# A fused attention and two-MLP kernel: other SBUF places for the last output copies of the first MLP and for two weight loads, and another slot for its last products

## The chip, the cores and the metric

The kernel runs on 1 core of one Trainium2 chip. The metric is the device time of one execution in microseconds (us). The kernel before takes 1925.05 us, the median of 3 runs (1924.63 to 1925.43).

## The reference, cut to what matters

```python
x = attention(q, k, v)                  # k and v mean-pooled by 8 along the sequence
x = x.transpose(0, 2, 1, 3).reshape(4608, 512)
h = sigmoid(x @ w_gate) * (x @ w_val)   # 512 -> 1536
x = h @ w_out                           # 1536 -> 512, first MLP
h = elu(x @ w_in2)                      # 512 -> 2048
out = h @ w_out2                        # 2048 -> 512, second MLP
```

There are 8 batches of 8 heads, 576 positions and 64 dimensions a head, so 4608 tokens of 512. The weights arrive as 64-bit floats and are read as pairs of 32-bit words.

## The kernel before, in words

All of it is one program, written in the order in which each engine runs it. Every engine is a queue: an instruction that waits holds up all that is behind it on that engine. A matrix product is made of three products of two-part numbers (high with high, high with low, low with high), since each operand is split into a high part (ScalarE, L93) and a rest (GpSimd or VectorE, L94).

**Blocks of the first MLP.** The tokens go in 12 blocks of 384 (`n`). A block has 12 groups of hidden columns (`c`). For a group TensorE makes the gate product and the value product (12 matmuls each, L501), ScalarE the sigmoid, VectorE the product of both (L513), ScalarE and GpSimd split it into `g`, and TensorE adds the output product of the group before (12 matmuls, L520) into four PSUM tiles `acc`. The two PSUM tiles `gv` are used in turn, so a gate or value product starts only after L513 has read the product two before it. At the block's end `flush_y` (L531) copies the four `acc` tiles, two on ScalarE and two on VectorE, to SBUF tiles `yo` and stores each to DRAM.

**Narrowing the weights.** In the first block the weights of the first MLP are still being made: 36 pieces (`Job`), three for each group (gate, value, out). A piece is loaded raw (L125, L131), its magnitude is taken on ScalarE (`open_to`, L188), VectorE narrows it in four passes (L106, L110, L116, L120), and ScalarE and GpSimd split it. `convert` (L195) does one step: it issues loads two pieces ahead, opens the next piece, runs two passes of one piece and two of the next in turn, and splits the piece before. A raw piece lies in one of two places of the tag `raw`, or, for an even piece number up to 30, in one of the 12 places of the tag `wo`, which the finished output weights fill in the end (L179 to L182). The narrowed form in work lies in one of three places of the tag `nt` (L143). From the second block on, the weights of the second MLP are narrowed in the same way in the gaps (`prepared`, L217) and stored to DRAM; that is over before the last block, and the `nt` places are next used by `flush_o` (L904).

**The second MLP.** It runs over 6 pairs of blocks (`s`), 8 column groups (`q`) and 7 products (`k`) each; such a step is a slot, counted through by `slot`. `product` (L845) adds 6 matmuls into one of two PSUM banks; `ORDER` says which bank and whether it is opened anew. `behind` (L868) reads the bank after each product: a bank can be added to or opened again only when its reader is done. After product 0 ScalarE copies the bank to `p`; product 2 goes on in that bank; after product 2 come ScalarE's Relu and Exp (with a table load the first time) and VectorE's L863, and product 4 opens the bank again; after product 4 VectorE makes `c` (L880), ScalarE Relu and Exp of it, VectorE L863 and L883, and the next group's product 0 opens the other bank behind L883. Between the products TensorE runs matmuls from the list `fill` (`filler`, L840): in the first group the 12 output products (L520) of the first MLP's last group, later those of the second MLP (L896). Work in the dictionary `due` is called at the end of its slot; the last `flush_y` is due in slot 4. Three of the four places of the tag `row`, from which `flush_y` takes its `yo` tiles (L89, L533), are held by `t_p1`, `t_u2` and `t_u3` (L825) there.

Of the kernel before, what the change touches and what calls it, by code (L numbers as in the profile page):

```python
# [9 lines left out]
F32 = mybir.dt.float32  # L10
# [14 lines left out]
def fused_kernel(  # L25
# [25 lines left out]
    NT, DM = out.shape  # L51
    F1 = w_gate.shape[1] // 2
    F2 = w_in2.shape[1] // 2
    P = 128
# [4 lines left out]
    C1 = F1 // P  # L59
    C2 = F2 // P  # L60
    NB = 384
    NBLK = NT // NB
# [9 lines left out]
    act = ctx.enter_context(tc.tile_pool(name="act", bufs=1))  # L72
# [12 lines left out]
    def raw_tile(name):  # L85

        return act.tile([P, DM, 2], I32, name=name, tag="raw", bufs=2)

    def row_tile(name, n=512):  # L89
        return act.tile([P, n], F32, name=name, tag="row", bufs=4)  # L90
# [79 lines left out]
    def upto(step, n):  # L170
        n = min(n, len(jobs))
        while count[step] < n:
            yield jobs[count[step]]
            count[step] += 1

    def fetch_to(n):
        for job in upto("fetch", n):
            i = count["fetch"]
            if i % 2 or i > 3 * C1 - 6:  # L179
                job.raw = raw_tile("rw")  # L180
            else:
                job.raw = wts.tile([P, DM, 2], I32, name="rwo", tag="wo", bufs=C1)  # L182
            job.load(job.raw)
# [346 lines left out]

    def flush_y(n, acc):  # L531
        for m in range(KD):
            t = row_tile("yo", NB)  # L533
            if m % 2:
                nc.vector.tensor_copy(out=t, in_=acc[m])
            else:
                nc.scalar.activation(out=t, in_=acc[m], func=AF.Copy)
            nc.sync.dma_start(out=y_dram[n][:, m], in_=t)
# [66 lines left out]
    with tc.manual_schedule():  # L605
# [101 lines left out]
        def low():  # L707
            for f in lows:
                f()
            lows.clear()  # L710
# [27 lines left out]
        def load_pair(q):  # L738
            wp[q] = [wts.tile([P, 7, 256], F32R, name=f"wr{q}{i}", tag="wg", bufs=C1) for i in range(2)]
            for i in range(2):  # L740
                nc.sync.dma_start(out=f32(wp[q][i]), in_=w_dram[q][:, i])

        def load_wo2(c):
            if c < C1:
                wo2[c] = wts.tile([P, 2, DM], F32R, name=f"w2o{c}", tag="wo", bufs=C1)
            elif c % 2 == 0:
                t = wts.tile([P, 2, 2, DM], F32R, name=f"w2o{c}", tag="wg", bufs=C1)
                wo2[c], wo2[c + 1] = t[:, 0], t[:, 1]
            nc.sync.dma_start(out=f32(wo2[c]), in_=wo2_dram[c])
# [6 lines left out]
        for n in range(NBLK):  # L756
# [3 lines left out]
            for c in range(C1):  # L760
# [49 lines left out]
                if pend is not None:  # L810
                    pn, pacc, pg, pc = pend
# [26 lines left out]
        fill = []  # L838

        def filler(n):  # L840
            for f in fill[:n]:
                f()
            del fill[:n]

        def product(k, q, flip, s):  # L845
            b, w, a, opens = ORDER[k]
            n = 0
            for j in range(2):
                for a_w, a_x in PASSES:
                    nc.tensor.matmul(  # L850
                        bank[b ^ flip], lhsT=wp[q][a_w][:, w, j * P:(j + 1) * P], rhs=form_tile(s, a)[j][:, a_x],
                        start=opens and n == 0, stop=n == 5, skip_group_check=True,
                    )
                    n += 1
# [13 lines left out]
        def behind(k, flip, g):  # L868
            src = bank[ORDER[k][0] ^ flip]
            u2 = t_u2  # L870
            if k == 0:
                nc.scalar.activation(out=t_p1, in_=src, func=AF.Copy)
            elif k == 1:
                nc.vector.tensor_tensor(out=u2, in0=t_p1, in1=src, op=ALU.add)  # L874
            elif k == 2:
                elu("c11", src, g)
            elif k == 3:
                nc.vector.tensor_tensor(out=t_u3, in0=t_p1, in1=src, op=ALU.add)
            elif k == 4:
                nc.vector.tensor_tensor(out=c_22, in0=t_u3, in1=src, op=ALU.add)  # L880
                elu("c22", c_22, g)
            elif k == 5:
                nc.vector.tensor_tensor(out=t_u3, in0=t_u3, in1=src, op=ALU.subtract)  # L883
                elu("c21", t_u3, g)
            else:
                nc.vector.tensor_tensor(out=u2, in0=u2, in1=src, op=ALU.add)
                elu("c12", u2, g)
# [3 lines left out]
        def to_out(acc, g, q, c, i, opens, closes):  # L891

            e, t = OUT_OF[c]

            def one(p, a_g, a_w):
                return lambda: nc.tensor.matmul(  # L896
                    acc[t + i], lhsT=g[c][:, a_g, i * P:(i + 1) * P], rhs=wo2[2 * q + e][:, a_w],
                    start=opens and p == 0, stop=closes and p == 2,
                )

            return [one(p, *x) for p, x in enumerate(PASSES)]

        def flush_o(t, acc):
            o = act.tile([P, DM], F32, name="po", tag="nt", bufs=3)  # L904
            if t % 2:
                nc.vector.tensor_copy(out=o, in_=acc)
            else:
                nc.scalar.activation(out=o, in_=acc, func=AF.Copy)
            nc.sync.dma_start(out=out[t * P:(t + 1) * P, :], in_=o)

        pn, pacc, pg, pc = pend
        fill += y_steps(pacc, pg, pc)
        NS = NBLK // 2
        prev = None
        flip = 0
        due = {4: [lambda: flush_y(pn, pacc)]}
        slot = 0
        for s in range(NS):
            for q in range(NQ):
                g = {  # L920
                    c: pool.tile([P, 2, NB], F32R, name="g" + c, tag=t, bufs=n)
                    for c, pool, t, n in (
                        ("c11", act, "g", 2), ("c12", mlp2[0], "g12", 1),
                        ("c21", mlp2[0], "g21", 1), ("c22", mlp2[0], "g22", 1),
                    )
                }
                if prev is not None:
                    ps_, pq, pg = prev
                    if pq == 0:
                        acc = [  # L930
                            ps.tile([P, DM], F32, name="oacc", tag="gv" if i < 2 else "acc", bufs=2 if i < 2 else 4)
                            for i in range(2 * TPB)
                        ]
                    if pq < NQ - 1:
                        for c in ("c11", "c22", "c21", "c12"):
                            for i in range(TPB):
                                fill += to_out(acc, pg, pq, c, i, pq == 0 and c in ("c11", "c22"), False)
                    else:
                        for n, i in enumerate((3, 4, 5, 0, 1, 2)):
                            for c in ("c11", "c12") if i < TPB else ("c21", "c22"):  # L940
                                fill += to_out(acc, pg, pq, c, i % TPB, False, c in ("c12", "c22"))
                            due.setdefault(slot + n + 1, []).append(
                                lambda t=ps_ * 2 * TPB + i, a=acc[i]: flush_o(t, a)
                            )
                for k in range(7):
                    product(k, q, flip, s)
                    filler(-(-len(fill) // max(1, (7 if slot > 6 else 5) - k)))
                    todo, later[:] = later[:], []
                    for f in todo:
                        f()  # L950
                    behind(k, flip, g)
                    low()
                    if k == 0 and (s > 0 or q > 0) and not (s == NS - 1 and q == NQ - 1):

                        load_pair((q + 1) % NQ)
                    if s == 0 and k == 1:
                        for c in {1: (10, 11), 2: (12, 13), 3: (14, 15)}.get(q, ()):
                            load_wo2(c)
                    if s + 1 < NS:
                        if q == 1 and k == 0:  # L960
                            load_raw(s + 1)
                        if q in (3, 4):
                            form_early(s + 1, (q - 3) * 7 + k)
                        if q == NQ - 1 and k == 4:

                            for i in range(8):
                                due.setdefault(slot + i, []).append(
                                    lambda i=i, s=s: form(s + 1, 3 + i // 2, i % 2)
                                )
                    for f in due.pop(slot, ()):  # L970
                        f()
                    slot += 1
                prev = (s, q, g)
                flip ^= 1
# [40 lines left out]
```

## Time and profile before

| what | value |
|---|---|
| median of 3 runs | 1925.05 us |
| the profiled execution, its own time | 1925.16 us |
| its span, first to last instruction | 1923.4 us |
| TensorE busy (matmul) | 1836.2 us, 95% |
| VectorE busy | 886.8 us, 46% |
| ScalarE busy | 810.7 us, 42% |
| GpSimd busy | 509.5 us, 26% |
| mean granted TensorE clock | 0.979 of full |
| DMA queue of the transfers | 211.84 MB, 32.4% of 16 engines |

Names are the engines' short forms: PE is TensorE, PEld its weight loads, DVE is VectorE, ACT is ScalarE, POOL is GpSimd, SP issues the DMAs. In a row of the timeline the first number is the start in us from the start of the span, the second the time from the first to the end of the last instruction that the row merges, `xN` their number, and the bracket the idle time before it and what ended it. Matmuls overlap, so six of them in 1.20 us are followed by the next after less than that.

### The profile page before, as it was taken

What the parts mean: (1) busy time and instruction counts of PE and PEld (TensorE: products, weight loads), DVE (VectorE), ACT (ScalarE), POOL (GpSimd) and SP (SyncE); (2) the same over time, 40 slices, a digit from 0 to 9 for tenths busy, and PEclk for the clock granted to TensorE, in tenths of its full rate; (3) what the DMA queues carried; (4) which work ended last, traced back from release to release, by engine and by line L of the source; (5) the groups of instructions that cost most, each with busy time, mean ns of one, the idle gap of its engine ahead of it and who ended that gap; (6) DMA issues with size and microseconds to landing.
All of it is one profiled execution on the core that took longest, in us unless ns stands there. A gap on an engine that the chain in (4) does not pass through costs nothing.

```text
span 1923.4 us, 25809 instructions
## 1 busy us (share of the span) xinstructions
PE 1836.2 (95%) x9996; PEld 1733.8 (90%) x9996; DVE 886.8 (46%) x1455; ACT 810.7 (42%) x1575; POOL 509.5 (26%) x523
## 2 busy tenths in 40 slices
PE   4676999999999999999999997999999999999999
PEld 3666999999999999999999997999999999999997
DVE  7987354554445544554422132544344344443432
ACT  3543344344444344444433224454454444544543
POOL 4444222222213132123222112222222222222222
PEclk7887999999999999999999999999999999999999
DMA  8332123232232322242210425334343343434330
GB/s 225 114 117 86 50 91 107 82 94 72 86 99 71 127 80 80 89 124 98 73 28 1 159 77 193 124 134 175 121 190 116 117 179 115 156 139 151 151 116 33
DMA packets 115771, 213.49 MB, mean 111 GB/s; under 512 B 43968, under 2 KB 72640, under 8 KB 115648
## 3 DMA queue, kind: packets, MB, share of 16 engines
q1 hardware_dynamic: 115648, 211.84, 32.4%
q8 instruction: 78, 1.28, 0.3%
q14 instruction: 45, 0.37, 0.1%
HBM read 169.87 MB, written 41.94 MB: 110 GB/s over the span
## 4 chain that ended last, share of the span: by engine, by line
PE 88%; DVE 7%; DMA 2%; ACT 2%; issue 1%; POOL 0%; SPq 0%; ACTq 0%; DVEq 0%; POOLq 0%
PE gv L501 28%; PE oacc L896 21%; PE bank L850 18%; PE acc L520 14%; PE xv L481 2%; PE ats L414 2%; PE atv L481 2%; DVE nt L106 1%; DVE ks L354 1%; DVE nt L116 1%; PE atq L404 1%; DVE nt L120 1%; PE att L454 1%; DMA rkv<-in_k_dram 1%; DVE nt L110 1%
## 5 line engine op out<-in xcount | busy, mean ns | idle before, releaser
L501 PE MATMUL gv<-x,wg 128*128 128x384 f32 x3456 | 651.8, 342 | 24.4 <-DVE sg L513 19.9
L501 PEld LDWEIGHTS gv<-x,wg 128*128 128x128 f32 x3456 | 607.0, 191 | 30.2 <-ACT wo L93 12.6
L896 PE MATMUL oacc<-w2o,gc 128*128 128x512 f32 x1728 | 452.9, 393 | 0.4 <-POOL gc L94 0.4
L896 PEld LDWEIGHTS oacc<-w2o,gc 128*128 128x128 f32 x1728 | 320.0, 188 | 48.4 <-POOL gc L94 0.8
L850 PE MATMUL bank<-form,wr 128*128 128x384 f32 x1728 | 354.0, 340 | 9.7 <-DVE u L883 8.3
L94 POOL TENSOR_TENSOR g<-sg,g 128x384 fp32r<-128x384 f32 x144 | 155.1, 1077 | 724.2 <-ACT g L93 724.2
L850 PEld LDWEIGHTS bank<-form,wr 128*128 128x128 f32 x1728 | 315.4, 188 | 32.9 <-DVE u L883 8.6
L520 PE MATMUL acc<-g,wo 128*128 128x384 f32 x1728 | 330.3, 339 | 2.0 <-POOL g L94 2.0
L520 PEld LDWEIGHTS acc<-g,wo 128*128 128x128 f32 x1728 | 304.4, 190 | 6.1 <-POOL g L94 3.4
L513 DVE TENSOR_TENSOR sg<-sg,gv 128x384 f32<-128x384 f32 x144 | 79.1, 549 | 313.8 <-PE gv L501 311.6
L94 POOL TENSOR_TENSOR gc<-ea,gc 128x384 fp32r<-128x384 f32 x96 | 98.0, 1021 | 301.5 <-ACT gc L93 297.3
L94 POOL TENSOR_TENSOR gc<-eb,gc 128x384 fp32r<-128x384 f32 x96 | 97.9, 1020 | 266.6 <-ACT gc L93 246.1
L509 ACT ACTIVATE sg<-gv 128x384 f32<-128x384 f32 x144 | 70.7, 491 | 199.9 <-PE gv L501 195.4
L93 ACT ACTIVATE g<-sg 128x384 fp32r<-128x384 f32 x144 | 75.6, 525 | 174.2 <-DVE sg L513 174.2
L859 ACT ACTIVATE ea<-bank 128x384 f32<-128x384 f32 x48 | 23.6, 492 | 158.5 <-PE bank L850 158.5
L94 DVE TENSOR_TENSOR pt<-att,pt 128x512 fp32r<-128x512 f32 x72 | 34.8, 486 | 114.7 <-ACT pt L93 114.7
L863 DVE SCALAR_TENSOR_TENSOR ea<-ea,bank 128x384 f32<-128x384 f32 x48 | 26.6, 555 | 118.0 <-ACT ea L860 118.0
L859 ACT ACTIVATE eb<-c 128x384 f32<-128x384 f32 x48 | 25.2, 525 | 129.6 <-DVE c L880 129.6
L93 ACT ACTIVATE gc<-eb 128x384 fp32r<-128x384 f32 x96 | 50.4, 525 | 56.3 <-DVE eb L863 33.0
L93 ACT ACTIVATE gc<-ea 128x384 fp32r<-128x384 f32 x96 | 50.5, 526 | 55.4 <-DVE ea L863 55.4
L874 DVE TENSOR_TENSOR u<-p,bank 128x384 f32<-128x384 f32 x48 | 26.6, 555 | 98.7 <-PE bank L850 97.3
L509 ACT ACT_TABLE_LOAD x34 | 43.6, 1283 | 49.8 <-PE gv L501 49.6
(104 smaller groups left out, 1872.5 us busy)
## 6 DMA issues: line engine op xcount, KB each, us to landing
wr<-wd SPq DMA_DIRECT2D x96, 896.0 KB, 6.3
rw<-in_moe_w_out_dram SPq DMA_DIRECT2D x23, 512.0 KB, 3.7
yd<-yo SPq DMA_DIRECT2D x48, 192.0 KB, 2.1
r<-yd SPq DMA_DIRECT2D x24, 384.0 KB, 8.4
out_dram<-po SPq DMA_DIRECT2D x36, 256.0 KB, 2.0
rw<-in_moe_w_in_dram SPq DMA_DIRECT2D x16, 512.0 KB, 4.5
wd<-rw SPq DMA_DIRECT2D x16, 512.0 KB, 3.5
wod<-rw SPq DMA_DIRECT2D x16, 512.0 KB, 2.8
```

What stands on the lines that cost most here:

```text
L93: nc.scalar.activation(out=dst_hi, in_=src, func=AF.Copy)
L94: eng.tensor_tensor(out=dst_lo, in0=src, in1=f32(dst_hi), op=ALU.subtract)
L414: nc.tensor.matmul(a[o:o + n, j // 2, (j % 2) * w:(j % 2 + 1) * w], lhsT=qt[:, j * P + o:j * P + o + n], rhs=kbd[b % 2][:, j * w:(j + 1) * w],
L481: nc.tensor.matmul(d[j][:, o:o + w], lhsT=vb[:m, a_w].rearrange("p e d -> p (e d)"), rhs=p[:m, a_p, j + e, o:o + w], start=(e == 0 and a_w ...
L501: nc.tensor.matmul(d, lhsT=w[:, i, a_w, j], rhs=x[:, a_x, j], start=(j == 0 and a_w == 0 and a_x == 0), stop=(j == KD - 1 and a_w == 1),)
L509: nc.scalar.activation(out=sg, in_=gps, func=AF.Sigmoid)
L513: nc.vector.tensor_tensor(out=sg, in0=sg, in1=vps, op=ALU.mult)
L520: return lambda: nc.tensor.matmul(acc[m], lhsT=wo[c][:, a_w, m * P:(m + 1) * P], rhs=g[:, a_g], start=(c == 0 and a_w == 0 and a_g == 0), ...
L850: nc.tensor.matmul(bank[b ^ flip], lhsT=wp[q][a_w][:, w, j * P:(j + 1) * P], rhs=form_tile(s, a)[j][:, a_x], start=opens and n == 0, stop= ...
L859: nc.scalar.activation(out=e, in_=src, func=AF.Relu, scale=-1.0)
L863: nc.vector.scalar_tensor_tensor(out=e, in0=e, scalar=-1.0, in1=src, op0=ALU.add, op1=ALU.max)
L896: return lambda: nc.tensor.matmul(acc[t + i], lhsT=g[c][:, a_g, i * P:(i + 1) * P], rhs=wo2[2 * q + e][:, a_w], start=opens and p == 0, st ...
```

## The change

Three edits: the even pieces 32 and 34 are also loaded into places of `wo`; in the flush of the last block the second to fourth copy go to `nt` places; the 12 output products that lay between the products 0 to 4 of the second MLP's first group all stand behind product 3, and the flush is due in slot 3 and not 4. After slot 6 `filler` counts as before.

```diff
     def fetch_to(n):
         for job in upto("fetch", n):
             i = count["fetch"]
-            if i % 2 or i > 3 * C1 - 6:
+            if i % 2:
                 job.raw = raw_tile("rw")
             else:
                 job.raw = wts.tile([P, DM, 2], I32, name="rwo", tag="wo", bufs=C1)
...
     def flush_y(n, acc):
         for m in range(KD):
-            t = row_tile("yo", NB)
+            if n == NBLK - 1 and m:
+                t = act.tile([P, DM], F32, name="yn", tag="nt", bufs=3)[:, :NB]
+            else:
+                t = row_tile("yo", NB)
...
-        due = {4: [lambda: flush_y(pn, pacc)]}
+        due = {3: [lambda: flush_y(pn, pacc)]}
...
                 for k in range(7):
                     product(k, q, flip, s)
-                    filler(-(-len(fill) // max(1, (7 if slot > 6 else 5) - k)))
+                    filler(len(fill) if slot == 3 else -(-len(fill) // (7 - k)) if slot > 6 else 0)
```

On SP, the queue that issues the loads, these are the loads of the pieces 31 to 35 in the first block and the first of the second MLP. Before:

```order
L125 DMA rw<-in_moe_w_val_dram 128x4x256
L131 DMA rw<-in_moe_w_out_dram 128x1024
L125 DMA rw<-in_moe_w_gate_dram 128x4x256
L125 DMA rw<-in_moe_w_val_dram 128x4x256
L131 DMA rw<-in_moe_w_out_dram 128x1024
L125 DMA rw_1499<-in_moe_w_in_dram 128x4x256
```

The same loads in the changed kernel:

```order
L125 DMA rw<-in_moe_w_val_dram 128x4x256
L131 DMA rwo<-in_moe_w_out_dram 128x1024
L125 DMA rw<-in_moe_w_gate_dram 128x4x256
L125 DMA rwo<-in_moe_w_val_dram 128x4x256
L131 DMA rw<-in_moe_w_out_dram 128x1024
L125 DMA rw_1499<-in_moe_w_in_dram 128x4x256
```

The order is the same; pieces 32 and 34 go to `rwo`, a place of `wo`, so that the five loads use two places of each tag in turn.

On PE, at the start of the second MLP, this is what stands from the second of the old gaps on (`form_9758` is the operand of product 2, `form_9812` of product 3, `form_9862` of product 4). Before:

```order
L520 MATMUL acc<-g,wo_1342 128x384 x3
L850 MATMUL bank_9984<-form_9758,wr_9501 128x384 x2
L850 MATMUL bank_9984<-form_9758,wr_9502 128x384
L850 MATMUL bank_9984<-form_9758,wr_9501 128x384 x2
L850 MATMUL bank_9984<-form_9758,wr_9502 128x384
L520 MATMUL acc<-g,wo_1342 128x384 x2
L850 MATMUL bank_9985<-form_9812,wr_9501 128x384 x2
L850 MATMUL bank_9985<-form_9812,wr_9502 128x384
L850 MATMUL bank_9985<-form_9812,wr_9501 128x384 x2
L850 MATMUL bank_9985<-form_9812,wr_9502 128x384
L520 MATMUL acc<-g,wo_1342 128x384 x2
L850 MATMUL bank_9984<-form_9862,wr_9501 128x384 x2
```

The same place in the changed kernel, from product 2 on:

```order
L853 MATMUL bank_9984<-form_9758,wr_9501 128x384 x2
L853 MATMUL bank_9984<-form_9758,wr_9502 128x384
L853 MATMUL bank_9984<-form_9758,wr_9501 128x384 x2
L853 MATMUL bank_9984<-form_9758,wr_9502 128x384
L853 MATMUL bank_9985<-form_9812,wr_9501 128x384 x2
L853 MATMUL bank_9985<-form_9812,wr_9502 128x384
L853 MATMUL bank_9985<-form_9812,wr_9501 128x384 x2
L853 MATMUL bank_9985<-form_9812,wr_9502 128x384
L520 MATMUL acc<-g,wo_1342 128x384 x12
L853 MATMUL bank_9984<-form_9862,wr_9501 128x384 x2
```

The products 0 to 3 now stand one behind another, and all 12 output products stand between product 3 and product 4. Lines behind `flush_y` have numbers higher by 3.

On DVE, in the same group, from the first L863 on. Before:

```order
L863 SCALAR_TENSOR_TENSOR ea<-ea,bank_9984 128x384
L878 TENSOR_TENSOR u_9988<-p_9986,bank_9985 128x384
L880 TENSOR_TENSOR c_9989<-u_9988,bank_9984 128x384
L535 COPY yo<-acc 128x384 x2
L863 SCALAR_TENSOR_TENSOR eb<-eb,c_9989 128x384
L883 TENSOR_TENSOR u_9988<-u_9988,bank_9985 128x384
```

The same place in the changed kernel:

```order
L866 SCALAR_TENSOR_TENSOR ea<-ea,bank_9984 128x384
L881 TENSOR_TENSOR u_9988<-p_9986,bank_9985 128x384
L538 COPY yn<-acc 128x384 x2
L883 TENSOR_TENSOR c_9989<-u_9988,bank_9984 128x384
L866 SCALAR_TENSOR_TENSOR eb<-eb,c_9989 128x384
L886 TENSOR_TENSOR u_9988<-u_9988,bank_9985 128x384
```

The two flush copies move from behind `c` to ahead of it. On ScalarE its two copies move likewise, from behind the Exp of `eb` to ahead of the Relu of `eb`. GpSimd's queue is unchanged.

## Rows read from the trace of the kernel before

**Rows 1.** Windows: start:end, length, busy time (instructions) by engine, PE clock, DMA share, GB/s
```profile
191.80:1148.90 957.10, 955.11 (x5689) 940.37 (x5688) 419.11 (x674) 372.21 (x701) 225.31 (x248) 1.00 0.27 85
1160.20:1168.40 8.20, 0.01 (x1) 0.00 (x0) 2.03 (x4) 0.91 (x2) 0.00 (x0) 0.77 0.21 75
1168.40:1172.30 3.90, 3.83 (x12) 3.50 (x13) 1.49 (x4) 2.73 (x6) 2.02 (x2) 0.61 0.95 328
1172.30:1923.40 751.10, 746.67 (x3691) 671.84 (x3690) 305.07 (x552) 344.54 (x700) 192.86 (x189) 1.00 0.37 139
```
**Rows 2.** Waits of PE, 1172 us to the end: us in total, times, longest
```profile
PE oacc L896 <- POOL gc L94: 0.4, 1, 0.4
```
**Rows 3.** Waits of all engines, 160 to 191.8 us
```profile
PE gv L501 <- DVE sg L513: 9.6, 3, 7.9
ACT nt L188 <- DMA rw<-in_moe_w_gate_dram: 5.5, 1, 5.5
```
**Rows 4.** Timeline, 130 to 143 us, a round of three pieces in the first block
```profile
130.54 0.41 DVE L106 TENSOR_SCALAR nt<-nt 128x512 f32<-128x512 f32 x1
...
131.92 0.69 DVE L116 SCALAR_TENSOR_TENSOR nt<-rw,nt 128x512 int32<-128x512 int32 x1
132.29 1.46 POOL L94 TENSOR_TENSOR wg<-nt,wg 128x512 fp32r<-128x512 f32 x1 [5.23 <-ACT wg L93]
132.53 1.50 DVE L106 TENSOR_SCALAR nt<-nt 128x512 f32<-128x512 f32 x1
...
135.58 2.32 PE L501 MATMUL gv<-x,wg 128*128 128x384 f32 x12 [1.18 <-DVE sg L513]
...
139.15 1.07 DVE L373 TENSOR_REDUCE vs<-v 128x64 f32<-128x512 f32 x1
...
142.91 0.69 DVE L116 SCALAR_TENSOR_TENSOR nt<-rwo,nt 128x512 int32<-128x512 int32 x1
```
**Rows 5.** Timeline, 163 to 190 us, the end of the first block
```profile
163.64 2.66 PE L520 MATMUL acc<-g,wo 128*128 128x384 f32 x12
...
169.22 0.69 DVE L116 SCALAR_TENSOR_TENSOR nt<-rw,nt 128x512 int32<-128x512 int32 x1
...
176.24 4.18 PE L501 MATMUL gv<-x,wg 128*128 128x384 f32 x12 [7.86 <-DVE sg L513]
...
189.54 2.35 PE L501 MATMUL gv<-x,wg 128*128 128x384 f32 x12 [1.25 <-DVE sg L513]
```
**Rows 6.** Timeline, 1148 to 1183 us, the start of the second MLP
```profile
1148.98 1.20 PE L850 MATMUL bank<-form,wr 128*128 128x384 f32 x6
...
1152.10 1.20 PE L850 MATMUL bank<-form,wr 128*128 128x384 f32 x6
...
1156.45 1.33 PE L850 MATMUL bank<-form,wr 128*128 128x384 f32 x6 [1.41 <-DVE ea L863]
...
1157.96 2.24 PE L850 MATMUL bank<-form,wr 128*128 128x384 f32 x12
...
1166.92 0.56 DVE L535 COPY yo<-acc 128x384 f32<-128x384 f32 x1 [4.52 <-DMA yd<-yo]
...
1167.86 0.55 DVE L883 TENSOR_TENSOR u<-u,bank 128x384 f32<-128x384 f32 x1
...
1168.47 2.29 PE L850 MATMUL bank<-form,wr 128*128 128x384 f32 x6 [8.26 <-DVE u L883]
...
1172.36 1.22 PE L850 MATMUL bank<-form,wr 128*128 128x384 f32 x6
...
1172.88 0.47 ACT L872 ACTIVATE p<-bank 128x384 f32<-128x384 f32 x1
...
1174.57 1.23 PE L850 MATMUL bank<-form,wr 128*128 128x384 f32 x6
...
1179.01 1.23 PE L850 MATMUL bank<-form,wr 128*128 128x384 f32 x6
...
1182.51 0.55 DVE L883 TENSOR_TENSOR u<-u,bank 128x384 f32<-128x384 f32 x1
```

## The prediction, as recorded before the changed kernel ran

> **What bounds the kernel now.** I read the windows by stage first, then the waits of TensorE, then the timeline at the two places where TensorE stands still. Between 191.8 and 1148.9 us TensorE is busy 955.1 of 957.1 us at the full granted clock, and from 1172.3 us to the end 746.7 of 751.1 us [rows 1]; in that last stretch the waits of TensorE that the trace names come to 0.4 us [rows 2]. So in these two stretches, nine tenths of the span, only fewer or shorter matmuls would help, and the change takes none away. It also means that whatever time is won before such a stretch is kept: everything behind it is in TensorE's pace and moves forward as a whole. What is left are two holes, and each edit lies at one of them.
>
> The first hole is the end of the first block. There ScalarE, opening piece 33, waits 5.5 us for its raw load [rows 3]; the trace has three such waits, one each for the pieces 33, 34 and 35. These pieces share two raw places, and a load can go out only when the piece two before has had its last pass. TensorE waits at the end of that chain, 9.6 us in three waits, 7.9 of it in one [rows 3].
>
> The second hole is the start of the second MLP: TensorE waits 1.41 us for L863 ahead of product 4 and 8.26 us for L883 ahead of the next group's product 0 [rows 6]. In the second wait VectorE does almost nothing (2.0 of 8.2 us busy, [rows 1]): its second copy for the flush stands 4.52 us waiting for a store [rows 6]. The four copies share one place of `row`, the other three being held, so copy and store alternate, and L863 and L883 stand behind the copies on VectorE.
>
> **The loads (first edit).** Pieces 32 and 34 go to `wo`, so load 33 no longer waits for piece 31 and load 35 no longer for piece 33; loads then go out as far ahead as in the rounds before. The places exist: ten of twelve are held by output weights and by piece 30 when load 32 is issued. Up to the pass L116 at 169.22 us nothing moves, because VectorE gets there on other work (the transposed probabilities come just ahead of it). From there I take the pace of an undisturbed round. In such a round TensorE's product that waits for L513 starts 135.58 − 131.92 = 3.66 us after the pass L116 [rows 4]. At the end of the block the same pair stands 176.24 − 169.22 = 7.02 us apart [rows 5]; this product moves to 172.88. A whole round takes 142.91 − 131.92 = 10.99 us, with a pooling step of 1.07 us that does not come again here, so 9.92 [rows 4]: the last piece's L116 starts at 179.14. From it to TensorE's last gate product it is 3.66 less the two passes of a following piece, which there is not (1.50 and about 0.41, as the long and the short pass of rows 4): 1.75, or 1.1 more if a pass of the last piece is held up by GpSimd. That gives 180.9 to 182.0. TensorE itself needs, from 172.88 on, a product at the slow pace (4.18), an output product (2.66) and a gate product (2.35, [rows 5]), which ends at 182.1 with all overlaps left out. I take 182.0. It now starts at 189.54 [rows 5]: **7.5 us**.
>
> Bounds: if every one of the 14 passes from there took the long 1.50 us, with 0.55 for L513, the last product could start only near 191.5, a loss of 2 us; if none did, TensorE's own products with their overlaps still fill the time to about 181.5, a gain of 8.0. I take the undisturbed round, since the same order of passes is measured there with the long and the short ones in it.
>
> A pass beside GpSimd shows what can be late next: L106 took 0.41 us alone and 1.50 us when it started behind a 1.46 us GpSimd split [rows 4]. The Trainium skill (SBUF — State Buffer, section Who interferes with whom) says that a VectorE instruction with two SBUF inputs, or one in a two-port mode, and a GpSimd instruction that reads SBUF do not share the port pair, but that the later waits for the earlier. By that rule the closer pace puts more passes behind splits; with all of them held the sum would lose these 7.5 us and 2 more, with the measured round it keeps them.
>
> **The twelve products and the flush (second and third edit).** Counted on from the first product at 1148.98 us, which nothing moves. Six matmuls take 2.24 − 1.20 = 1.04 us in a row, one 0.17 [rows 6]. Without fill product 2 starts at 1151.06; it needs the copy of product 0, which is done at 1150.18 + 0.47, so it does not wait. From product 2 to product 4 it is 1156.45 − 1152.10 = 4.35 us, the chain of Relu, table load, Exp and L863 [rows 6]. That chain stays, and sets product 4 to 1155.41. Beside it TensorE has the products 2 and 3 and all twelve, 4 × 1.04 = 4.16 us: its wait shrinks from 1.41 to 0.2 us. So the early products gain 1.04 us, and two more output matmuls are already done.
>
> The four copies now have four places: the three of `nt` are idle (no instruction between 960 us and the flush names them), the fourth is the free one of `row`. They stand ahead of `c` on VectorE and ahead of the Relu of `eb` on ScalarE. Two of 0.56 us behind L863 and L878 end near 1156.8; `c` cannot start before product 4 has ended, 1156.7, so they cost 0.1 us. From product 4 to L883, without a flush between them, it is 1182.51 − 1179.01 = 3.50 us, one group later [rows 6]; L883 then runs 1159.0 to 1159.56, and the next group's product 0 follows at 1159.6 instead of 1168.47. TensorE runs out of work at 1155.41 + 3 × 1.04 = 1158.5, so a wait of 1.1 us stays.
>
> Late next is ScalarE's copy of that product: it ends 4.94 us after L883 (1173.35 against 1168.41), in an order that stays, so at 1164.5, and product 2 of that group follows at 1164.54; TensorE could be there at about 1164.2. Now it starts at 1174.57 [rows 6]: **10.0 us**. Of this the low clock behind the long wait is a part: with 0.61 granted, product 0 and its fill of six took 3.89 us up to 1172.36, the next product and its fill of five at the full clock 2.21 [rows 1, 6].
>
> Bounds: at most both waits and the slow start go, 1.41 + 8.26 + 1.5 = 11.1 us; at least, were the copies held as before, 1.1 us.
>
> The transfers behind the flush on SP (weights of the group after next, the next rows of the first MLP) go out some 9 to 10 us earlier, and so does their use; they keep about the same time to land.
>
> **Sum.** 7.5 + 10.0 = 17.5 us from the profiled execution's 1925.16 us (0.1 above the median, span 1923.4) gives **1907.6 us**.
>
> **The rivals.** *The first block stays bound by VectorE and GpSimd.* The holes in the loads close, but the passes and the splits hold each other up until nothing is won. For it: passes three times as long beside a split [rows 4]. Against it: the rounds before run at that pace with both engines as busy. 1925.16 − 10.0 = 1915.1 us. Half of it would be 1911.4.
>
> *The flush waits on as before.* The copies still stall VectorE, because a place of `nt` comes free late or a store holds the next. Then only the 1.1 us ahead of product 4 are won there: 1925.16 − 7.5 − 1.1 = 1916.6 us. Against it: nothing has used `nt` for nearly 200 us.
>
> *Slower: TensorE's clock.* Bare products with a wait behind several of them keep the granted clock at half from 1148 us on, and the groups after that never bring it back. A slot takes 2.21 us at the full clock [rows 6], a group of seven 15.5; at half it costs 15.5 more. From 1.4 groups on (17.5 + 3.9 us lost) the kernel is slower; two groups give 1907.6 + 31 = 1938.6 us. Against it: the longest waits left are near 1 us, and behind 8.26 us the clock is at 0.61 for four us and then at 1.00 [rows 1]. The Trainium skill (TensorE: Matmul & The Clock Gate, section HAM oscillation — how this bites in real kernels) warns of such a pattern, bursts between waits that bring the clock back to half each time; the trace shows the fall, but only behind waits of many us.
>
> **How the numbers follow.** The forecast has 0.84, the first rival 0.08 (half of it lies inside the range), the flush 0.04, the clock 0.02; 0.02 is left for both gains failing together. A measurement of this kernel can tell about 0.2%, 3.9 us, from no change. All but the last two cases are faster by more: 0.96 faster, 0.02 same, 0.02 slower. The range goes from 1905.0 (8.0 + 11.1 us won, and about 1 us for the spread and for durations rounded here) to 1912.0 (half of the first gain missing, and 0.6).
>
> **What would show it.** In the profile after: no wait of ScalarE for a raw load at 160 to 190 us, and the last gate product of the first block near 182; products 0 to 3 bare, product 4 some 6.4 us after product 0, four copies without a wait for a store, and the next group's product 0 some 10.6 us after the first product instead of 19.5; the granted clock at 1.00 all through. The forecast is wrong if a new wait of some us stands ahead of that last gate product, or if the two stretches that TensorE fills grow longer than 957.1 and 751.1 us.

## The result, and the profile after

The changed kernel takes 1908.77 us, the median of 4 runs (1907.54 to 1909.53), beside 1925.24 us for the kernel before on the same chip (4 runs, 1924.63 to 1925.72). The ratio is 0.9914 with a 95% interval of 0.9897 to 0.9931: 16.5 us faster, where 17.5 were forecast (1907.6 us). The profiled execution took 1908.89 us, with a span of 1907.2 us against 1923.4.

First the windows of the profile after, in the same columns as [rows 1]. The second and the last row answer to the first and the last there.

```profile
160.00:184.40 24.40, 18.88 (x77) 17.87 (x77) 21.13 (x29) 10.93 (x19) 12.71 (x10) 0.73 0.27 87
184.40:1141.50 957.10, 955.86 (x5693) 941.40 (x5694) 418.06 (x672) 372.38 (x702) 227.15 (x248) 1.00 0.27 85
1141.50:1151.00 9.50, 9.48 (x55) 9.16 (x54) 5.66 (x10) 5.02 (x9) 2.19 (x2) 1.00 0.01 3
1151.00:1156.00 5.00, 4.26 (x23) 3.68 (x22) 2.12 (x5) 3.57 (x7) 1.36 (x2) 1.00 1.00 336
1156.00:1907.20 751.20, 746.66 (x3691) 671.16 (x3689) 306.02 (x552) 345.21 (x702) 193.79 (x190) 1.00 0.38 139
```

In the two long stretches TensorE has kept its pace: in windows laid equally long it is busy 955.86 of 957.10 us and 746.66 of 751.20, against 955.11 of 957.10 and 746.67 of 751.10 in [rows 1]. How long the stretches themselves are is read between the same instructions, at the end of this section. What was won lies outside them, in the two holes. At the start of the second MLP TensorE is now busy 9.48 of 9.50 us and then 4.26 of 5.00, all at a granted clock of 1.00, where before it stood still for 8.20 us and then ran at 0.61.

The waits of all engines from 160 to 195 us (us in total, times, longest):

```profile
PE gv L501 <- DVE sg L513: 5.5, 3, 4.3
...
ACT nt L188 <- POOL wo L94: 2.4, 2, 1.2
ACT nt L188 <- POOL wg L94: 1.6, 1, 1.6
```

ScalarE's L188 waits for no load any more; the three waits for raw pieces that [rows 3] came from are gone, and what stands in their place is short and on GpSimd's split. TensorE's three waits there fell from 9.6 to 5.5 us, the longest from 7.9 to 4.3. The timeline of the same end of the first block:

```profile
171.01 0.69 DVE L116 SCALAR_TENSOR_TENSOR nt<-rwo,nt 128x512 int32<-128x512 int32 x1
...
174.65 4.18 PE L501 MATMUL gv<-x,wg 128*128 128x384 f32 x12 [4.34 <-DVE sg L513]
...
178.32 0.69 DVE L116 SCALAR_TENSOR_TENSOR nt<-rwo,nt 128x512 int32<-128x512 int32 x1
...
181.41 0.69 DVE L116 SCALAR_TENSOR_TENSOR nt<-rw,nt 128x512 int32<-128x512 int32 x1
182.13 1.66 DVE L120 SCALAR_TENSOR_TENSOR nt<-rw,nt 128x512 int32<-128x512 int32 x1
...
184.40 2.32 PE L501 MATMUL gv<-x,wg 128*128 128x384 f32 x12 [0.74 <-DVE sg L513]
```

From the pass L116 of piece 32 to the last gate product it is 184.40 − 171.01 = 13.39 us; in [rows 5] it was 189.54 − 169.22 = 20.32. That is 6.93 us won. The start of the second MLP, to be laid beside [rows 6]:

```profile
1142.74 4.32 PE L853 MATMUL bank<-form,wr 128*128 128x384 f32 x24
1146.90 2.25 PE L520 MATMUL acc<-g,wo 128*128 128x384 f32 x12
1149.16 3.40 PE L853 MATMUL bank<-form,wr 128*128 128x384 f32 x18
1149.49 1.01 DVE L538 COPY yn<-acc 128x384 f32<-128x384 f32 x2
1149.57 0.47 ACT L540 ACTIVATE yo<-acc 128x384 f32<-128x384 f32 x1
1149.94 0.48 ACT L540 ACTIVATE yn<-acc 128x384 f32<-128x384 f32 x1
1150.52 0.56 DVE L883 TENSOR_TENSOR c<-u,bank 128x384 f32<-128x384 f32 x1
...
1152.70 0.55 DVE L886 TENSOR_TENSOR u<-u,bank 128x384 f32<-128x384 f32 x1
1153.30 1.31 PE L853 MATMUL bank<-form,wr 128*128 128x384 f32 x6 [0.74 <-DVE u L886]
...
1157.71 0.47 ACT L875 ACTIVATE p<-bank 128x384 f32<-128x384 f32 x1
1158.24 1.31 PE L853 MATMUL bank<-form,wr 128*128 128x384 f32 x6
```

Products 0 to 3 are one row of 24 matmuls, the twelve output products one row behind them, and the four copies go out within 1 us without a bracket, so none waits for a store. From the group's first product to product 2 of the next group it is 1158.24 − 1142.74 = 15.50 us, before 1174.57 − 1148.98 = 25.59: 10.09 us won.

The spans differ by 16.2 us. The two holes give 6.93 + 10.09 = 17.02. Between the last gate product and the first product of the second MLP after takes 958.34 us and before 959.44 (1.10 won), behind the second hole 748.96 and 748.83 (0.13 lost). And the pass of piece 32 starts at 171.01 instead of 169.22 us, 1.79 lost ahead of that pass, where the engines do the same work as before (a second execution of the changed kernel, below, has it at 169.03): 17.02 + 1.10 − 0.13 − 1.79 = 16.2.

### The profile page after: what moved, and what is told of

It reads as the page before. It is cut to its first block, busy times and chain, and to the rows that moved or that the text cites. A ratio compares the mean times of both kernels' runs of the same rounds, so it can differ in the third digit from the quotient of the medians.

```text
span 1907.2 us, 25809 instructions
## 1 busy us (share of the span) xinstructions
PE 1833.6 (96%) x9996; PEld 1731.5 (91%) x9996; DVE 887.2 (47%) x1455; ACT 811.4 (43%) x1575; POOL 510.1 (27%) x523
## 4 chain that ended last, share of the span: by engine, by line
PE 89%; DVE 7%; ACT 1%; issue 1%; DMA 1%; SPq 0%; POOL 0%; ACTq 0%; DVEq 0%; POOLq 0%
PE gv L501 29%; PE oacc L899 21%; PE bank L853 18%; PE acc L520 14%; PE ats L414 2%; PE xv L481 2%; PE atv L481 2%; DVE nt L106 2%; DVE nt L116 1%; DVE ks L354 1%; PE atq L404 1%; DVE nt L120 1%; PE att L454 1%; DVE nt L110 1%; DMA rkv<-in_k_dram 0%
## 5 line engine op out<-in xcount | busy, mean ns | idle before, releaser
L866 DVE SCALAR_TENSOR_TENSOR ea<-ea,bank 128x384 f32<-128x384 f32 x48 | 26.6, 555 | 116.4 <-ACT ea L863 116.4
```

## The experiments

The theory was the prediction's: two independent gains, the loads (first edit) and the copies (second edit), with the moved products (third edit) worth about one us. Its rivals were that the first block stays bound by VectorE and GpSimd, and that the flush stalls on. The first four kernels ran together (before: 1925.34 us, 21 runs), the last three together (before: 1926.19 us, 12 runs).

**First edit alone.**

```diff
-            if i % 2 or i > 3 * C1 - 6:
+            if i % 2:
```

> Only the first edit: raw pieces 32 and 34 go to places of wo, the flush and the twelve products as before. Theory (each hole has its own edit and the gains add): ScalarE's three waits for raw loads go, the last gate product of the first block comes 6.5 to 7.5 us earlier against the pass L116 of piece 32, and all that gain is kept: about 1918 us against about 1925, with the 8.3 us wait of TensorE at the second MLP's start unchanged. Rival (the first block stays bound by VectorE and GpSimd, and the whole gain came from the second hole): about 1925. Rival (the loads also help the second hole by shifting transfers): below 1916.

Measured: 1919.82 us (1917.88 to 1920.00), ratio 0.9966 (0.9954 to 0.9979). Its timeline at the end of the first block and at the start of the second MLP:

```profile
168.95 0.69 DVE L116 SCALAR_TENSOR_TENSOR nt<-rwo,nt 128x512 int32<-128x512 int32 x1
...
172.59 4.18 PE L501 MATMUL gv<-x,wg 128*128 128x384 f32 x12 [4.46 <-DVE sg L513]
...
182.33 2.35 PE L501 MATMUL gv<-x,wg 128*128 128x384 f32 x12 [0.81 <-DVE sg L513]
...
1161.15 2.29 PE L850 MATMUL bank<-form,wr 128*128 128x384 f32 x6 [8.24 <-DVE u L883]
```

The first hole closes as in the full change (pass L116 at 168.95, so 13.38 us to 182.33), and the second stays as it was, with its wait of 8.24 us. By the medians the edit wins 5.5 us (by the interval 4.0 to 8.9), by the trace 6.94; the profiled execution, 1917.88 us, is the fastest of its five. The rival that sees no gain in the first block falls, and so does the one below 1916 us.

**Second edit alone.**

```diff
-            t = row_tile("yo", NB)
+            if n == NBLK - 1 and m:
+                t = act.tile([P, DM], F32, name="yn", tag="nt", bufs=3)[:, :NB]
+            else:
+                t = row_tile("yo", NB)
```

> Only the second edit: the last flush's copies 2 to 4 go to nt places; loads, the spread of the twelve products and the flush's slot as before. Theory: the single place was the wait. Product 0 of the second group follows L883 some 11.7 us after the first product instead of 19.5, product 2 of that group comes 9.0 us earlier, about 1916 us; the 1.4 us wait ahead of product 4 stays. Rival (the copies in VectorE's and ScalarE's queues ahead of L863 are themselves the wait, whatever their places): the wait stays over 5 us, about 1922 or more.

Measured: 1916.91 us (1915.54 to 1917.78), ratio 0.9953 (0.9941 to 0.9966). Its timeline at the start of the second MLP:

```profile
1149.62 1.20 PE L853 MATMUL bank<-form,wr 128*128 128x384 f32 x6
...
1157.08 1.32 PE L853 MATMUL bank<-form,wr 128*128 128x384 f32 x6 [1.41 <-DVE ea L866]
...
1158.91 1.01 DVE L538 COPY yn<-acc 128x384 f32<-128x384 f32 x2
...
1161.22 1.31 PE L853 MATMUL bank<-form,wr 128*128 128x384 f32 x6 [0.39 <-DVE u L886]
...
1166.16 1.31 PE L853 MATMUL bank<-form,wr 128*128 128x384 f32 x6
```

The wait of 8.26 us has become 0.39, although the copies still stand behind `c`; the 1.41 us ahead of product 4 stay. From the first product (1149.62) to product 2 of the next group (1166.16) it takes 16.54 us, before 25.59: 9.05 of the 10.09 come from the places alone. The rival of the flush falls.

**Third edit alone**, so that all four copies still share one place.

```diff
-        due = {4: [lambda: flush_y(pn, pacc)]}
+        due = {3: [lambda: flush_y(pn, pacc)]}
...
-                    filler(-(-len(fill) // max(1, (7 if slot > 6 else 5) - k)))
+                    filler(len(fill) if slot == 3 else -(-len(fill) // (7 - k)) if slot > 6 else 0)
```

> Only the third edit: all twelve products behind product 3 and the flush due in slot 3, but the copies still share the one place of row. Theory: the copies, now ahead of c on VectorE, hold c back by three round trips of copy and store (2.5 us each); TensorE's long wait moves from the second group's product 0 to product 6 of the first group and is about 7 us; all in all 1 to 2 us won, about 1923.5 us. Rival (placing the flush early frees the place in time and the wait goes): about 1916. Rival (the copies ahead of c cost more than the late ones): 1927 or more.

Measured: 1922.61 us (1921.74 to 1924.13), ratio 0.9986 (0.9977 to 0.9996). Its timeline at the start of the second MLP:

```profile
1148.59 4.32 PE L850 MATMUL bank<-form,wr 128*128 128x384 f32 x24
...
1155.42 0.47 ACT L537 ACTIVATE yo<-acc 128x384 f32<-128x384 f32 x1
1157.88 0.56 DVE L535 COPY yo<-acc 128x384 f32<-128x384 f32 x1 [2.45 <-DMA yd<-yo]
1160.40 0.49 ACT L537 ACTIVATE yo<-acc 128x384 f32<-128x384 f32 x1 [4.51 <-DMA yd<-yo]
1162.95 0.56 DVE L535 COPY yo<-acc 128x384 f32<-128x384 f32 x1 [4.52 <-DMA yd<-yo]
...
1164.03 4.10 PE L850 MATMUL bank<-form,wr 128*128 128x384 f32 x12 [6.65 <-DVE c L880]
```

Here the stall of the second hole can be read piece by piece: each copy starts about 2.5 us after the one before, when that one's store has landed, and VectorE holds `c` behind its second copy. The wait has only moved, from the next group's product 0 to product 6, which needs the bank that `c` reads. The hole is 22.96 us (2.63 won, where 1 to 2 were expected): an order without places is worth little. The rivals, that the wait goes or that the kernel slows down, both fall.

**Half of the first edit**: piece 32 loads as before, only piece 34 goes to a place of `wo`.

```diff
-            if i % 2 or i > 3 * C1 - 6:
+            if i % 2 or i == 3 * C1 - 4:
```

> Half of the first edit: piece 34 goes to wo, piece 32 stays in raw, all else as before. Theory (a load waits for the last pass of the piece two before in its place): load 33 still waits for piece 31, so the first wait of ScalarE (5.5 us) stays and the other two go; the last gate product comes about half of the full edit's gain earlier, 3 to 4 us, about 1921.7 us. Rival (any one place more is enough): as the full edit, about 1918. Rival (all hangs on the first wait): no gain, about 1925.

Measured: 1921.50 us (1920.19 to 1925.34), ratio 0.9983 (0.9974 to 0.9991). One wait of ScalarE for a load is left, the gate piece 33, in its list of waits:

```profile
ACT nt L188 <- DMA rw<-in_moe_w_gate_dram: 5.6, 1, 5.6
```

The hole is 16.68 us (186.06 − 169.38), 3.64 won of the 6.93. With piece 34 in `wo` load 34 goes out right behind load 33 (169.49 and 169.07 us), and load 35 waits for the last pass of piece 32 and no longer for that of piece 33. The other half, 3.29 us, is piece 32's, which frees load 33, but by subtraction: piece 32 alone in `wo` was not run.

**The flush in slot 4**, all else as changed.

```diff
-        due = {3: [lambda: flush_y(pn, pacc)]}
+        due = {4: [lambda: flush_y(pn, pacc)]}
```

> The changed kernel with the flush due in slot 4 as before (copies behind c on VectorE and behind the Exp of eb on ScalarE); loads, places and the twelve products as in the changed kernel. Theory (with four places the copies lie beside ScalarE's Relu and Exp in either slot): the next group's product 0 starts within 0.3 us of where it does in the changed kernel, 10.6 us after the first product; the time is the same as the changed kernel's within 1 us, about 1908.5. Rival (the earlier slot is part of the gain): the copies hold L863 and L883 back by their 1 us, and the time is 1 us or more longer.

Measured: 1908.39 us (1907.36 to 1909.29), ratio 0.9907 (0.9891 to 0.9922); the changed kernel itself, beside it, below, has 1907.97. The copies go back behind `c` (VectorE's two start at 1151.40), and the next group waits as long for VectorE as after (0.74):

```profile
1153.71 1.31 PE L853 MATMUL bank<-form,wr 128*128 128x384 f32 x6 [0.73 <-DVE u L886]
```

Once the copies have places, it doesn't matter on which side of `c` they stand: the hole is 15.52 us, and the rival of a longer time falls. So the third edit's share, 16.54 − 15.50 = 1.04 us, is that of the moved products.

**The changed kernel again**, without an edit, as the yardstick of this group.

> The changed kernel once more, unaltered. Its profile had the passes of piece 32 start 1.8 us later than the kernel before, though nothing ahead of them differs; the first three score products of the attention ran at the slow pace there. Theory (that is a difference from run to run): the start of that pass lies anywhere between 168.8 and 171.0 us here, its distance to the block's last gate product is again 13.4 us, and product 2 of the second group again starts 15.5 us after the first product; the time is 1906 to 1910. Rival (the change itself delays the start): the pass starts at 170.8 to 171.2 again.

Measured: 1907.97 us (1907.11 to 1908.51), ratio 0.9906 (0.9892 to 0.9919). Its timeline at the end of the first block:

```profile
167.05 0.67 DVE L116 SCALAR_TENSOR_TENSOR nt<-rw,nt 128x512 int32<-128x512 int32 x1
...
169.03 0.69 DVE L116 SCALAR_TENSOR_TENSOR nt<-rwo,nt 128x512 int32<-128x512 int32 x1
...
182.43 2.32 PE L501 MATMUL gv<-x,wg 128*128 128x384 f32 x12 [0.89 <-DVE sg L513]
```

First hole 13.40 us (169.03 to 182.43), second 15.49, span 1906.0. The pass of piece 32 starts at 169.03 and not near 171, so the rival that the change itself delays it falls.

**The splits of the first block's weights on VectorE** in place of GpSimd. What was open was why the first hole came out 0.6 us longer than forecast: the theory put it to passes that wait beside GpSimd's splits, the rival to VectorE's own work.

```diff
-            split(hi, lo, t.bitcast(F32))
+            split(hi, lo, t.bitcast(F32), nc.vector)
```

> The changed kernel, but in the first block the rest of each narrowed piece (L94, the second half of the split) is made on VectorE and not on GpSimd, 36 instructions; the output is the same. Theory (passes that wait behind GpSimd's splits, 1.50 against 0.41 to 0.68 us, set the pace of the first block): the long passes go, at 1.7 of them for a piece some 1.8 us, and 0.55 to 0.7 us a piece is added on VectorE; a round of three pieces takes about 9 us and not 9.9, and the kernel 5 to 15 us less: 1894 to 1904. Rival (VectorE's own work sets the pace, and the long passes lie beside waits for ScalarE): the added 36 instructions lengthen the block by up to 20 us, 1915 to 1928.

Measured: 1921.19 us (1920.46 to 1922.06), ratio 0.9975 (0.9965 to 0.9986): still faster than before, but 13.2 us slower than the changed kernel beside it. Its timeline of a round of three pieces, and then of the end of the first block:

```profile
142.06 0.69 DVE L94 TENSOR_TENSOR wg<-nt,wg 128x512 fp32r<-128x512 f32 x1 [0.37 <-ACT wg L93]
...
143.28 0.42 DVE L106 TENSOR_SCALAR nt<-nt 128x512 f32<-128x512 f32 x1
...
146.07 0.68 DVE L116 SCALAR_TENSOR_TENSOR nt<-rwo,nt 128x512 int32<-128x512 int32 x1
146.79 1.17 POOL L94 TENSOR_TENSOR g<-sg,g 128x384 fp32r<-128x384 f32 x1 [10.20 <-ACT g L93]
147.00 1.50 DVE L120 SCALAR_TENSOR_TENSOR nt<-rwo,nt 128x512 int32<-128x512 int32 x1
...
157.21 0.69 DVE L116 SCALAR_TENSOR_TENSOR nt<-rw,nt 128x512 int32<-128x512 int32 x1
...
178.52 0.67 DVE L116 SCALAR_TENSOR_TENSOR nt<-rw,nt 128x512 int32<-128x512 int32 x1
...
181.44 0.68 DVE L116 SCALAR_TENSOR_TENSOR nt<-rwo,nt 128x512 int32<-128x512 int32 x1
...
194.92 3.88 PE L501 MATMUL gv<-x,wg 128*128 128x384 f32 x12 [1.84 <-DVE sg L513]
```

The passes do get short (0.42 us, where the changed kernel's L106 has a median of 1.49 from 60 us on), and the one split that stays on GpSimd still lies beside a long one (1.50). But each of the 36 rests costs VectorE 0.69 us, and about 0.36 us of waiting for ScalarE's copy ahead of it. A round with its pooling step takes 157.21 − 146.07 = 11.14 us; the same three pieces take 146.21 − 135.22 = 10.99 in the changed kernel again. So a round is no shorter: a rest costs about as much, 0.69 + 0.36 = 1.05 us, as the held pass that it saves, 1.50 − 0.42 = 1.08.

The loss is in the pieces that had no held pass, where the rest is only added: the one ahead of piece 32 takes 181.44 − 178.52 = 2.92 us instead of 169.03 − 167.05 = 1.98. Up to the last piece's L116 the changed kernel again has 37 passes of over 1.2 us, about one a piece and not the 1.7 of the expectation; this kernel has 14. By these counts, as an estimate, 23 held passes fewer save 25 us and 35 rests at 0.94 (2.92 − 1.98) to 1.05 us cost 33 to 37, a loss of 8 to 12; the last L116 comes 191.51 − 179.43 = 12.08 us later, and the block's last gate product starts at 194.92 instead of 182.43. The theory fell, the rival's range held: the held passes are there, but taking the splits off GpSimd buys no time. The work only changes engine, and VectorE is the one that has none to spare (13.14 of 13.39 us busy in the first hole after).

## Why the prediction held, by its steps

**The two long stretches.** "Whatever time is won before such a stretch is kept" held to about 1 us. Between the same products the first stretch takes 958.34 us where it took 959.44, the second 748.96 where it took 748.83. The first six experiments have 958.90 to 959.87 in the first stretch, those with the full loads edit on both sides of the kernel before; the changed kernel again has 959.14. So the 1.10 us cannot be put down to the change.

**The loads: 7.5 us forecast, 6.93 measured.** The mechanism was right, the term too large by 0.6. The first piece of the sum, from L116 to the product that waits for it, was 3.66 and came out 174.65 − 171.01 = 3.64. The round was taken at 9.92 and took 181.41 − 171.01 = 10.40. Four of its passes were held (1.49 to 1.50 us), but so were four in the round of [rows 4] (1.50, 1.52, 1.50 and 1.33 us); what differs is its third piece, right behind the pooling step:

```profile
139.64 1.29 POOL L94 TENSOR_TENSOR wg<-nt,wg 128x512 fp32r<-128x512 f32 x1 [1.30 <-ACT wg L93]
140.14 1.33 DVE L116 SCALAR_TENSOR_TENSOR nt<-rw,nt 128x512 int32<-128x512 int32 x1
```

There half a microsecond of the split ran under the pooling step, and the piece took 142.91 − 140.14 = 2.77 us; without the pooling step it takes 181.41 − 178.32 = 3.09. And the pooling step, taken out with its 1.07 us, had put the next pass off by only 140.14 − 139.15 = 0.99. So a step can't be taken out of a measured round by its own length when another engine works under it. At the end, where the working had 1.75 us or 1.1 more, the last piece's L120 was held (1.66 us) and it took 2.99: the upper case. The statement on the granted clock was too wide: it said 1.00 all through, which is so in the second hole, but from 160 us to the last gate product it was 0.73 (before 0.69). The working had its slow product of 4.18 us in that stretch and counted with it; TensorE waits for VectorE there.

The rule that the prediction weighed, of a VectorE instruction that waits for a GpSimd one at the shared port (the Trainium skill, SBUF — State Buffer, section Who interferes with whom), agrees with the lengths of the passes in the last experiment: L106 takes 0.42 us with no split beside it, and L120 1.50 when it starts while the one split left on GpSimd runs. That all of them would be held, and the gain lost, didn't happen.

**Product 4.** Forecast 6.43 us after the first product with a wait of 0.2 left; it came at 1149.16 − 1142.74 = 6.42, with a wait of TensorE's weight load on L866 of 0.3.

**The copies.** Forecast to end 7.8 us after the first product; 7.76 measured. `c` was to be 0.1 us late, and in the experiment with the flush in slot 4 the next group starts no earlier. L886 was to run from 10.02 to 10.58 us after the first product; 9.96 to 10.51 measured. The wait of TensorE behind it was forecast at 1.1 us and is 0.74.

**Late next.** ScalarE's copy of the next group's product 0 was forecast 15.5 us after the first product and ends at 15.44 (1158.18), with product 2 at 15.50 where 15.56 was forecast. This step mattered: TensorE has work from 1153.30 on, but only this copy lets the group go on. **10.0 us forecast, 10.09 measured.**

**The sum.** 17.5 forecast, 17.0 in the two holes. Nothing ties the rest of the difference between the two profiles to the change: the pass of piece 32 started 1.79 us later than in the profile before, and 1.10 us came back between the holes. In eight profiles whose engines do the same work ahead of that pass (before, after and the first six experiments) it starts anywhere from 168.79 to 171.01 us.

**The rivals.** The first block did not stay bound (first edit alone), the flush did not wait on (second edit alone), and the clock did not fall: 1.00 across both windows behind the first product. But the prediction's reading that it falls only behind waits of many us was too narrow: in the first block of the kernel before, 12 matmuls at 146.57 us took 3.47 us behind a wait of 2.19, at a granted clock of 0.63, where at 1.00 they take 2.25. The edits hardly touch each other: the holes of the first two, each alone, closed by 6.94 (20.32 − 13.38) and 9.05 us, with the third 1.04 more, against 17.02 together.

## What to carry to other kernels

When an engine's wait ends with a load or a store, count the places that the tiles of that tag rotate through before moving any instruction: two loads or four copies that share places too few take turns with their transfers, and everything queued behind them on the engine pays. Tiles that have gone idle by then are places that cost nothing; here they brought 16 of the 17 us, the new order one. Add up a gain by the next thing that is late (here ScalarE's copy of the following product), not by the wait that goes.

## What the runs showed of the hardware that was not expected

**The start differs by run, and the clock rows there did not show it.** The 24 matmuls L414 of the first scores, all ahead of any change, are as follows (shortest, median and longest ns, then first and last start). The profile after:

```profile
L414 PE MATMUL ats<-kbd,qt x24: 444/447/580, 16.3 to 25.9; 128*128 128x144 f32 x24
...
0.00:30.00 30.00, 12.74 (x46) 10.05 (x46) 17.24 (x26) 10.41 (x20) 6.32 (x14) 1.00 0.72 203
```

The changed kernel again:

```profile
L414 PE MATMUL ats<-kbd,qt x24: 286/286/444, 16.5 to 23.7; 128*128 128x144 f32 x24
...
0.00:30.00 30.00, 10.15 (x46) 7.85 (x46) 18.02 (x28) 11.30 (x23) 7.07 (x15) 0.90 0.79 217
```

In the profile after none of them is shorter than 444 ns, and the granted clock of that window reads 1.00; in the repeat, with a median of 286 ns, it reads 0.90. So in this window the durations tell more than the clock's column, and the kernel's mean clock (0.990 after, 0.984 in the repeat) isn't to be read as a faster run: its pass of piece 32 comes 1.98 us later (171.01 against 169.03). What makes the start slow in one execution and not in the next was not tried.
